# Projecting both heads of a chunk in one matmul against a block diagonal omega of 128 by 256

## The chip, the cores and the metric

The kernel runs on one core of a Trainium2 chip. The metric is the device time of one execution in microseconds (us), from the first to the last instruction and what the launch adds around them. Engines are named as in the profile: PE is TensorE doing matmuls, PEld its weight loads, DVE is VectorE, ACT is ScalarE, POOL is GpSimd and SP is the sync engine, which here only issues DMAs.

## The reference

Two stages follow each other. The first is linear attention with positive random features: 8 batches, 8 heads, 576 positions, head dimension 64, 128 features. The second is a gated feed-forward layer over the 4608 tokens (model width 512, hidden width 1536), which takes the attention's output as its input.

```python
def phi(x):                                # x is q or k, scaled by 1/sqrt(sqrt(64))
    proj = np.einsum('bhsd,md->bhsm', x, omega)      # 64 -> 128 features
    sq = np.sum(x * x, axis=-1, keepdims=True) / 2.0
    h = proj - sq
    h = h - np.max(h, axis=-1, keepdims=True)
    return np.exp(h) / np.sqrt(m)
kv = einsum('bhsm,bhsd->bhmd', phi(k), v);  z = phi(k).sum(axis=2)
num = einsum('bhsm,bhmd->bhsd', phi(q), kv)
den = einsum('bhsm,bhm->bhs', phi(q), z) + 1e-6
x = (num / den), heads side by side        # 4608 x 512
out = (silu(x @ w_gate) * (x @ w_val)) @ w_out
```

## The kernel before, in words

**Groups, steps, chunks.** The attention works on groups. A group is 256 rows (two chunks of 128, `CH = 2`) of two neighbouring heads of one batch, of q or of k. There are 72 groups of k and 72 of q. A step takes two groups, so there are 72 steps: six with k alone, sixty with one of q and one of k, six with q alone. Heads of one pair lie side by side: after the transposes, `x[:, i, ...]` has the 64 dimensions of the pair's first head in partitions 0 to 63 and those of its second head in partitions 64 to 127.

**What one step does to its two groups.** `load` brings the rows (L369, L376). `st_transpose` turns four chunks of 128 by 128 on PE (L411), squares the rows on POOL (L418) and copies the result to `x` on ACT (L419). `st_project` multiplies by omega (L434): for each group `i`, chunk `c` and head `hh` one matmul whose weights are 64 rows of `x` and whose moving operand is 64 rows of `omT`, 128 columns wide. That is eight matmuls a step in plain fp32. `omT` holds omega's transpose twice, once in partitions 0 to 63 and once in 64 to 127 (L337 to L348), so the first head uses the array's upper 64 rows and the second its lower 64 rows. The results go to two PSUM banks of 512 columns: `pp0` takes the first head of both groups, `pp1` the second head. In the profile each fp32 matmul shows as two weight loads and two matmul records, so a step has 16 records on L434.

`st_max` takes the sum of squares (L448) and, for each bank, the largest of 128 features (L455), both on DVE, and forms the bias in two small operations (L457, L458). `st_exp` writes `ph`, eight exponentials of 128 by 128 on ACT (L470), with a bias per row. A step's exponentials therefore wait for both maxima.

After that, k's `ph` is multiplied with v into `kvacc` (L572, two steps later), and q's `ph` is transposed (L596) and multiplied with the sums (`q_mult` L613, or in later batches `q_out` L653, whose weights are 64 columns wide and whose moving operand has 256 columns). `q_out` also transposes the finished rows in the early batches (L646).

**What sets the order.** The calls of a step are written out in two lists: `CLOSE`, for the steps before the first two tiles of 512 tokens are whole, and `GROUPED`, after that, in which pieces of the feed-forward layer (`SHARE`) stand between the attention's calls. The feed-forward's matmuls are in fp32r with 512 columns: gate and value L689, down L698, and in the last part, in a seven-product scheme, L928. A planner decides by fixed costs how much of it is given to each step. The order that an engine finally gets is made when the program is built, by a scheduler that may move an instruction past others of its engine. Weights of the feed-forward are converted by ACT and POOL (L251, L252, L277 to L295) beside it.

**PSUM.** Eight banks: three for `ps_moe`, two for `pp` (`ps_proj`), one each for the transposes (`ps_tr`), for the products (`ps_att`) and for `kvacc`. In odd early steps `pp` is taken from `ps_moe`.

Of the kernel before, what the change touches and what calls it, by code (L numbers as in the profile page):

```python
# [11 lines left out]
F32 = mybir.dt.float32  # L12
# [3 lines left out]
AF = mybir.ActivationFunctionType  # L16
ALU = mybir.AluOpType
AX = mybir.AxisListType
# [5 lines left out]
def kernel(  # L24
# [11 lines left out]
    nc = tc.nc  # L36
    B, H, S, D = q.shape
    M = omega.shape[0]
    NT, DM = out.shape
    DF = w_gate.shape[1]  # L40
    P = 128
# [6 lines left out]
    CH = G // P  # L48
# [4 lines left out]
    SCALE = 1.0 / math.sqrt(math.sqrt(D))  # L53
# [27 lines left out]
    const = ctx.enter_context(tc.tile_pool(name="const", bufs=1))  # L81
# [25 lines left out]
    def ps_moe(name, shape):  # L107
        return ps_m.tile(shape, F32, name=name, tag="m")
# [228 lines left out]

    omT = const.tile([P, M], F32, name="omT")  # L340

    def setup_omega():
        om2 = accp.tile([P, 2, D], F32, name="om2", tag="acc")
        for j in range(2):
            nc.scalar.dma_start(om2[:, j, :], omega)
        pt = ps_moe("pt_om", [P, M])
        nc.tensor.transpose(pt, om2.rearrange("p a d -> p (a d)"), ident)
        nc.scalar.activation(omT, pt, AF.Copy, scale=SCALE)  # L348

# [71 lines left out]
    def st_project(n):  # L423
        if n >= NS:
            return
        x, st, sq = sts[n]

        new = ps_moe if n < EARLY and n % 2 else ps_proj
        pp = [new(f"pp{hh}_{n}", [P, 2, CH, M]) for hh in range(2)]
        for i in range(2):  # L430
            for c in range(CH):
                for hh in range(2):
                    r = slice(hh * D, (hh + 1) * D)
                    nc.tensor.matmul(  # L434
                        pp[hh][:, i, c, :], x[r, i, c * P : (c + 1) * P], omT[r], start=True, stop=True
                    )
        sts[n] = st, sq, pp
        return True

# [2 lines left out]
    def st_max(n):  # L442
        if n >= NS:
            return
        st, sq, pp = sts[n]

        with tc.issue_after(biased[0].ins) if biased else ExitStack():
            nc.vector.tensor_reduce(  # L448
                st[:, 0].rearrange("p i c h -> p (i c h)"),
                sq.rearrange("p i c h d -> p (i c h) d"),  # L450
                axis=AX.X,
                op=ALU.add,
            )
        for hh in range(2):
            nc.vector.tensor_reduce(st[:, 1, :, :, hh], pp[hh], axis=AX.X, op=ALU.max, negate=True)  # L455
        s0, s1, s2, s3 = (st[:, j].rearrange("p i c h -> p (i c h)") for j in range(4))
        nc.vector.scalar_tensor_tensor(s2, s0, SQC, s1, op0=ALU.mult, op1=ALU.add)  # L457
        biased[:] = [nc.vector.scalar_tensor_tensor(s3, s0, -SQC, s2, op0=ALU.mult, op1=ALU.add)]  # L458
        step_end["v"] = biased[0]
        return True  # L460

    def st_exp(n):
        if n >= NS:
            return
        st, _, pp = sts.pop(n)
        for i, (kind, b, g) in enumerate(steps[n]):
            ph = att.tile([P, CH, 2 * M], F32, name=f"ph{i}_{n}", tag=f"ph{i}", bufs=3)
            for hh in range(2):
                for c in range(CH):
                    step_end["s"] = nc.scalar.activation(  # L470
                        ph[:, c, hh * M : (hh + 1) * M], pp[hh][:, i, c, :],
                        AF.Exp, bias=st[:, 3, i, c, hh : hh + 1], scale=1.0,
                    )
            box[kind, b, g] = ph
        return True
# [591 lines left out]
    def give(us):  # L1067
# [16 lines left out]
    SHARE = None  # L1084
    CLOSE = (
        st_project,
        q_norm,
        q_out,
        lambda n: st_transpose(n + 1),
        q_mult,  # L1090
        lambda n: k_accumulate(n, 0),
        st_max,
        q_transpose,
        lambda n: k_accumulate(n, 1),
        st_exp,
        q_den,
    )
    GROUPED = (
        q_out,
        st_project,  # L1100
        q_transpose,
        lambda n: k_accumulate(n, 0),
        lambda n: k_accumulate(n, 1),
        st_max,
        st_exp,
        q_den,
        lambda n: st_transpose(n + 1),
# [10 lines left out]
    for n in range(2):  # L1118
        load(n)
        if n == 0:  # L1120
            setup_omega()
# [64 lines left out]
```

## Time and profile before

| | |
|---|---|
| median of 3 runs | 1171.24 us (1169.88 to 1176.55) |
| the profiled execution | 1174.65 us, of which its span is 1172.6 us |
| PE busy, and weight loads | 1145.0 us (98%), 948.3 us (81%) |
| DVE, ACT, POOL busy | 703.3, 684.7, 588.6 us |
| first and last projection matmul | 6.4 and 546.4 us |

How to read the profile: a record of PE covers a matmul from its start to its modelled end, and matmuls overlap in the pipeline. So what a matmul costs PE is not its duration but how much later the next one starts. The timeline merges neighbouring records of one line and tile into one row: its first number is the start of the first, its second the time from there to the end of the last, and x16 says how many were merged. The distance from one row's start to the next row's start is then what the whole row took of PE. "64*128" in a PE row is the weights' rows and columns, "64x128" the moving operand's rows and columns. The column PEclk of the stages is the granted clock, 1.00 for full.

### The profile page before, as it was taken

The numbers are of one execution on the slowest core, as the hardware profiler recorded it, in microseconds if no ns is written. First come the engines' busy times: TensorE is split into PE (matmuls) and PEld (weight loads), VectorE is DVE, ScalarE is ACT, GpSimd is POOL, SyncE is SP. The second block draws the span as 40 slices with busy tenths as digits, with TensorE's granted clock in tenths as the row PEclk, the third lists the DMA queues.
The fourth block names the chain that finished last, engine by engine and source line by source line (L and its number), as shares of the span: only waits on it lengthen the run. The fifth ranks groups of instructions, "written<-read, shape, count | busy, mean of one in ns | idle before, by whom it ended". The sixth has DMA issues, their size and how long they took to land.

```text
span 1172.6 us, 18833 instructions
## 1 busy us (share of the span) xinstructions
PE 1145.0 (98%) x6633; PEld 948.3 (81%) x6633; DVE 703.3 (60%) x1266; ACT 684.7 (58%) x1541; POOL 588.6 (50%) x515
## 2 busy tenths in 40 slices
PE   8999999999999999999999999999999999999998
PEld 7888778888787778767778788888878888888886
DVE  3777576454666665556373566666566666456654
ACT  4888887877766866857434544444444445444441
POOL 3332353253656775586335655544455543555551
PEclk9999999999999999999999999999999999999999
DMA  6655355654445543431445111124211111211103
GB/s 141 160 135 132 102 161 142 185 151 122 129 130 139 143 140 102 109 86 55 135 109 151 57 55 55 54 65 124 63 50 46 52 52 46 81 55 54 46 18 72
DMA packets 173965, 114.30 MB, mean 97 GB/s; under 512 B 125840, under 2 KB 144304, under 8 KB 173872
## 3 DMA queue, kind: packets, MB, share of 16 engines
q1 hardware_dynamic: 172528, 112.78, 35.1%
q8 instruction: 52, 0.85, 0.3%
q10 hardware_dynamic: 1344, 0.33, 0.1%
q14 instruction: 41, 0.34, 0.1%
HBM read 87.88 MB, written 25.18 MB: 96 GB/s over the span
## 4 chain that ended last, share of the span: by engine, by line
PE 80%; DVE 7%; ACT 4%; POOL 3%; DMA 3%; issue 2%; SPq 0%; POOLq 0%; DVEq 0%; ACTq 0%
PE o L698 22%; PE a L928 16%; PE c L928 8%; PE g L689 6%; PE pp L434 6%; PE kvacc L572 5%; PE v L689 4%; PE d L928 4%; PE pt L411 3%; PE po L613 3%; PE ptq L596 2%; ACT ph L470 2%; PE xt L653 1%; POOL wlo L252 1%; PE xt L646 1%
## 5 line engine op out<-in xcount | busy, mean ns | idle before, releaser
L470 ACT ACTIVATE ph<-pp,st 128x128 f32<-128x128 f32 x576 | 157.3, 387 | 12.8 <-DVE st L458 12.3
L728 DVE TENSOR_TENSOR acc<-o,acc 128x512 f32<-128x512 f32 x156 | 105.8, 685 | 94.6 <-PE o L698 94.2
L418 POOL TENSOR_TENSOR sq<-nat 128x512 f32<-128x512 f32 x72 | 78.1, 1084 | 156.2 <-DVE st L448 113.5
L915 POOL TENSOR_TENSOR wlo<-wspare,whi 128x512 fp32r<-128x512 f32 (+1 forms) x60 | 60.9, 1036 | 117.4 <-ACT whi L914 111.0
L455 DVE TENSOR_REDUCE st<-pp 128x4 f32<-128x512 f32 x144 | 92.8, 683 | 43.2 <-PE pp L434 42.8
L434 PE MATMUL pp<-omT,x 64*128 64x128 f32 x1152 | 96.0, 296 | 3.4 <-ACT x L419 2.3
L252 POOL TENSOR_TENSOR wlo<-wraw,whi 128x512 fp32r<-128x512 f32 x59 | 82.5, 1404 | 26.9 <-ACT whi L251 23.0
L434 PEld LDWEIGHTS pp<-omT,x 64*128 64x128 f32 x1152 | 78.2, 195 | 20.8 <-issue 10.1
L915 POOL TENSOR_TENSOR wlo<-s,whi 128x512 fp32r<-128x512 f32 x64 | 82.4, 1306 | 3.8 <-ACT whi L914 3.8
L1024 ACT COPY late<-a 128x512 f32<-128x512 f32 x72 | 42.2, 586 | 60.0 <-PE a L928 58.8
L698 PE MATMUL o<-whi,late 128*128 128x512 f32 x192 | 74.5, 389 | 0.0
L572 PE MATMUL kvacc<-v,ph 128*128 128x65 f32 x512 | 69.1, 276 | 0.0
L536 DVE TENSOR_REDUCE dj<-jk 128x4 f32<-128x512 f32 x36 | 24.6, 684 | 73.3 <-POOL jk L532 60.7
L572 PEld LDWEIGHTS kvacc<-v,ph 128*128 128x128 f32 x512 | 66.4, 200 | 0.5
L789 POOL TENSOR_TENSOR hl<-sl,hh 128x512 fp32r<-128x512 f32 x36 | 46.9, 1306 | 34.6 <-ACT hh L788 34.6
L291 POOL TENSOR_TENSOR wc<-st 128x512 int32<-128x512 int32 x36 | 37.4, 1040 | 47.7 <-ACT st L289 25.2
L419 ACT COPY x<-pt 128x512 f32<-128x512 f32 x72 | 43.2, 600 | 28.3 <-PE pt L411 26.9
L689 PE MATMUL g<-xh,whi 128*128 128x512 f32 x144 | 59.5, 414 | 0.0
L1028 DVE TENSOR_TENSOR late<-c,late 128x512 f32<-128x512 f32 x25 | 17.3, 692 | 69.7 <-PE c L928 60.6
L698 PE MATMUL o<-whi,hh 128*128 128x512 f32 x144 | 58.4, 406 | 0.5 <-ACT sl L765 0.4
L689 PE MATMUL v<-xh,whi 128*128 128x512 f32 x144 | 57.7, 401 | 0.0
L689 PE MATMUL g<-xh,wlo 128*128 128x512 f32 x144 | 57.4, 398 | 0.0
(255 smaller groups left out, 3355.7 us busy)
## 6 DMA issues: line engine op xcount, KB each, us to landing
wraw<-wscr SPq DMA_DIRECT2D x63, 256.0 KB, 2.7
wspare<-wscr SPq DMA_DIRECT2D x60, 256.0 KB, 2.7
wscr<-wc SPq DMA_DIRECT2D x36, 256.0 KB, 2.2
out_dram<-acc SPq DMA_DIRECT2D x72, 128.0 KB, 2.4
nat<-in_k_dram SPq DMA_DIRECT2D x64, 128.0 KB, 3.0
nat<-in_q_dram SPq DMA_DIRECT2D x64, 128.0 KB, 3.1
v<-in_v_dram SPq DMA_DIRECT2D x62, 128.0 KB, 3.6
st<-in_moe_w_gate_dram SPq DMA_DIRECT2D x12, 512.0 KB, 3.9
```

The costliest lines, as they stand in the source:

```text
L252: nc.gpsimd.tensor_tensor(lo, raw, hi.bitcast(F32), op=ALU.subtract)
L418: nc.gpsimd.tensor_tensor(sq, nat, nat, op=ALU.mult)
L434: nc.tensor.matmul(pp[hh][:, i, c, :], x[r, i, c * P : (c + 1) * P], omT[r], start=True, stop=True)
L455: nc.vector.tensor_reduce(st[:, 1, :, :, hh], pp[hh], axis=AX.X, op=ALU.max, negate=True)
L470: step_end["s"] = nc.scalar.activation(ph[:, c, hh * M : (hh + 1) * M], pp[hh][:, i, c, :], AF.Exp, bias=st[:, 3, i, c, hh : hh + 1], scal ...
L572: nc.tensor.matmul(acc[:, 2 * (pr % 2) + hh, :], ph[:, c, hh * M : (hh + 1) * M], vt[:, 2 * c + j if gr is None else c, hh, :], start=firs ...
L689: nc.tensor.matmul(ps, a_[:, ws], b_[:, c, :], start=n == 0, stop=n == 3 * NC - 1)
L698: nc.tensor.matmul(ps, a_[:, ts_], b_, start=first and n == 0, stop=last and n == 2)
L728: nc.vector.tensor_tensor(a_, po, a_, op=ALU.add)
L789: nc.gpsimd.tensor_tensor(hl, h, hh.bitcast(F32), op=ALU.subtract)
L915: nc.gpsimd.tensor_tensor(lo, src_, hi.bitcast(F32), op=ALU.subtract)
L928: nc.tensor.matmul(ps, a_[:, w_], b_[:, c, :], start=start and c == 0 and m == 0, stop=c == CH - 1 and m == 2, skip_group_check=True,)
```

## The change

`omT` becomes a tile of 128 by 2 by 128: partitions 0 to 63 hold omega's transpose in the first 128 columns and zeros in the second, partitions 64 to 127 the other way round. One matmul with all 128 rows of `x` as weights and all 256 columns of `omT` then gives both heads' features of a chunk. A step has four such matmuls in place of eight. The banks are dealt out anew: `pp0` takes the first group and `pp1` the second, each with both chunks and both heads; the maxima (two, of the same size as before) and the exponentials (eight, the same) read them accordingly. The setup gets two memsets on DVE and one more small activation on ACT.

```diff
-    omT = const.tile([P, M], F32, name="omT")
+    omT = const.tile([P, 2, M], F32, name="omT")
...
-        nc.scalar.activation(omT, pt, AF.Copy, scale=SCALE)
+        for j in range(2):
+            r = slice(j * D, (j + 1) * D)
+            nc.vector.memset(omT[r, 1 - j], 0.0)
+            nc.scalar.activation(omT[r, j], pt[r], AF.Copy, scale=SCALE)
...
-        pp = [new(f"pp{hh}_{n}", [P, 2, CH, M]) for hh in range(2)]
+        pp = [new(f"pp{i}_{n}", [P, CH, 2, M]) for i in range(2)]
         for i in range(2):
             for c in range(CH):
-                for hh in range(2):
-                    r = slice(hh * D, (hh + 1) * D)
-                    nc.tensor.matmul(
-                        pp[hh][:, i, c, :], x[r, i, c * P : (c + 1) * P], omT[r], start=True, stop=True
-                    )
+                nc.tensor.matmul(
+                    pp[i][:, c].rearrange("p h m -> p (h m)"),
+                    x[:, i, c * P : (c + 1) * P],
+                    omT.rearrange("p h m -> p (h m)"),
+                    start=True, stop=True,
+                )
...
-        for hh in range(2):
-            nc.vector.tensor_reduce(st[:, 1, :, :, hh], pp[hh], axis=AX.X, op=ALU.max, negate=True)
+        for i in range(2):
+            nc.vector.tensor_reduce(st[:, 1, i], pp[i], axis=AX.X, op=ALU.max, negate=True)
...
-                        ph[:, c, hh * M : (hh + 1) * M], pp[hh][:, i, c, :],
+                        ph[:, c, hh * M : (hh + 1) * M], pp[i][:, c, hh, :],
```

Lines after the projection move down by three or four in the changed kernel (L434 becomes L435, L470 becomes L474, L596 becomes L600 and so on). The built order moves as follows at three places.

On PE, at step 41 in the grouped part: the transposes of finished rows (`xt`), the projection (`pp0_41`, `pp1_41`), the transposes of q's features (`ptq`), the k products (`kvacc`) and the transposes of the next step (`pt_42`). Before:

```order
L646 MATMUL xt3_5_3584<-ident_90,xn3_5_3562 128x128 x2
L434 MATMUL pp0_41_3593<-omT_96,x_41_3515 128x128
L434 MATMUL pp1_41_3594<-omT_96,x_41_3515 128x128
L434 MATMUL pp0_41_3593<-omT_96,x_41_3515 128x128
L434 MATMUL pp1_41_3594<-omT_96,x_41_3515 128x128
L434 MATMUL pp0_41_3593<-omT_96,x_41_3515 128x128
L434 MATMUL pp1_41_3594<-omT_96,x_41_3515 128x128
L434 MATMUL pp0_41_3593<-omT_96,x_41_3515 128x128
L434 MATMUL pp1_41_3594<-omT_96,x_41_3515 128x128
L596 MATMUL ptq3_7_3603<-ident_90,ph0_40_3500 128x128 x4
```

The same place on PE in the changed kernel:

```order
L650 MATMUL xt3_5_3423<-ident_90,xn3_5_3401 128x128 x2
L435 MATMUL pp0_41_3432<-omT_96,x_41_3354 128x256 x2
L435 MATMUL pp1_41_3433<-omT_96,x_41_3354 128x256 x2
L600 MATMUL ptq3_7_3438<-ident_90,ph0_40_3339 128x128 x4
L576 MATMUL kvacc5_0_3445<-v0_97,ph1_39_3243 128x65 x4
L414 MATMUL pt_42_3465<-ident_90,nat42_3206 128x128 x4
```

The neighbours stay; the eight matmuls that took turns between two banks become two on one bank and two on the other.

On PE, at step 18 in the close part, where the built order puts q's products (`po`) between a step's first projection matmul and its others. Before:

```order
L596 MATMUL ptq1_1_1244<-ident_90,ph0_16_1181 128x128 x4
L572 MATMUL kvacc2_0_1024<-v3_100,ph1_15_1116 128x65 x2
L434 MATMUL pp0_18_1267<-omT_96,x_18_1222 128x128
L613 MATMUL po1_0_1227<-kvr1_0_668,qt1_0_1177 128x65 x4
L434 MATMUL pp1_18_1268<-omT_96,x_18_1222 128x128
L434 MATMUL pp0_18_1267<-omT_96,x_18_1222 128x128
L434 MATMUL pp1_18_1268<-omT_96,x_18_1222 128x128
L434 MATMUL pp0_18_1267<-omT_96,x_18_1222 128x128
L434 MATMUL pp1_18_1268<-omT_96,x_18_1222 128x128
L434 MATMUL pp0_18_1267<-omT_96,x_18_1222 128x128
L434 MATMUL pp1_18_1268<-omT_96,x_18_1222 128x128
L646 MATMUL xt1_0_1283<-ident_90,xn1_0_1235 128x128 x2
```

The same place on PE in the changed kernel:

```order
L600 MATMUL ptq1_1_1175<-ident_90,ph0_16_1116 128x128 x4
L576 MATMUL kvacc2_0_967<-v3_100,ph1_15_1055 128x65 x2
L435 MATMUL pp0_18_1198<-omT_96,x_18_1153 128x256
L617 MATMUL po1_0_1158<-kvr1_0_631,qt1_0_1112 128x65 x4
L435 MATMUL pp0_18_1198<-omT_96,x_18_1153 128x256
L435 MATMUL pp1_18_1199<-omT_96,x_18_1153 128x256 x2
L650 MATMUL xt1_0_1210<-ident_90,xn1_0_1166 128x128 x2
```

The split stays, now after one of four matmuls instead of one of eight. In the program before, 55 of the 72 steps have their eight matmuls in one piece and 17 in two; in the changed one 61 have their four in one piece.

On ACT, at step 41: copies of finished rows and of transposed features (`xo`, `qt`), the copy of the next step's transposes (`x_42`), and the exponentials (`ph0`, `ph1`). Before:

```order
L668 COPY xo3_5_4_3590<-xt3_5_3584 128x192
L598 COPY qt3_7_3608<-ptq3_7_3603 128x512
L419 COPY x_42_3635<-pt_42_3630 128x512
L470 ACTIVATE ph0_41_3620<-pp0_41_3593,st_41_3516 128x128 x2
L470 ACTIVATE ph0_41_3620<-pp1_41_3594,st_41_3516 128x128 x2
L470 ACTIVATE ph1_41_3625<-pp0_41_3593,st_41_3516 128x128 x2
L470 ACTIVATE ph1_41_3625<-pp1_41_3594,st_41_3516 128x128 x2
```

The same place on ACT in the changed kernel:

```order
L672 COPY xo3_5_4_3429<-xt3_5_3423 128x192
L602 COPY qt3_7_3443<-ptq3_7_3438 128x512
L474 ACTIVATE ph0_41_3455<-pp0_41_3432,st_41_3355 128x128 x4
L474 ACTIVATE ph1_41_3460<-pp1_41_3433,st_41_3355 128x128 x4
L422 COPY x_42_3470<-pt_42_3465 128x512
```

The first group's exponentials now read one bank and the second's the other, and the copy of the next step's `x` stands behind the exponentials instead of ahead of them. From step 25 on that is so in nearly every step; in the steps up to 24 the copy stands ahead in both kernels.

## The prediction

> **What bounds the kernel now.** I read the page first: the busy shares, then the chain that ended last.
>
> ```profile
> PE 1145.0 (98%) x6633; PEld 948.3 (81%) x6633; DVE 703.3 (60%) x1266; ACT 684.7 (58%) x1541; POOL 588.6 (50%) x515
> PE 80%; DVE 7%; ACT 4%; POOL 3%; DMA 3%; issue 2%; SPq 0%; POOLq 0%; DVEq 0%; ACTq 0%
> ```
>
> PE is busy nearly throughout and makes up four fifths of the chain. That is an average over stages, so I cut the span at the first feed-forward matmul (about 119 us) and where the attention is done (about 575 us). The columns are each engine's busy time and record count, then the granted clock and the DMAs.
>
> ```profile
> 0.00:25.00 25.00, 19.45 (x114) 17.15 (x114) 8.80 (x18) 10.52 (x31) 7.99 (x25) 1.00 0.68 155
> 25.00:119.00 94.00, 92.23 (x894) 84.51 (x894) 70.33 (x188) 79.99 (x246) 31.14 (x30) 1.00 0.57 138
> 119.00:575.00 456.00, 441.95 (x3031) 359.53 (x3031) 265.76 (x564) 328.60 (x792) 253.02 (x223) 1.00 0.45 125
> 575.00:1172.00 597.00, 591.35 (x2600) 487.08 (x2598) 358.45 (x498) 265.59 (x474) 296.43 (x238) 1.00 0.24 68
> ```
>
> In the two stages that hold 68 of the 72 projections (25 to 575 us) PE idles 94.00 - 92.23 + 456.00 - 441.95 = 15.8 us in all. Work added to PE there must lengthen the run, but for what fits in those 15.8 us. So the question is what the projection takes of PE now and what it will take. This is its row among the groups, with the two waits of PE and PEld ahead of it that the change can touch:
>
> ```profile
> L434 PE MATMUL pp<-omT,x 64*128 64x128 f32 x1152 | 96.0, 296 | 3.4 <-ACT x L419 2.3 <-ACT ph L470 1.0
> PEld pp L434 <- ACT ph L470: 3.1, 6, 1.2
> ```
>
> A mean of 296 ns for 1152 records would be 341 us if they ran one after another, and the group is busy for 96.0. Records overlap, so durations don't price it; distances between starts do. Step 41, PE alone:
>
> ```profile
> 274.85 0.38 PE L646 MATMUL xt<-ident,xn 128*128 128x128 f32 x2
> 275.16 1.16 PE L434 MATMUL pp<-omT,x 64*128 64x128 f32 x16
> 276.25 0.66 PE L596 MATMUL ptq<-ident,ph 128*128 128x128 f32 x4
> ```
>
> Sixteen records take 276.25 - 275.16 = 1.09 us, 0.068 each. Step 18, with its split, gives the reference for full-array matmuls:
>
> ```profile
> 85.30 0.48 PE L434 MATMUL pp<-omT,x 64*128 64x128 f32 x2
> 85.71 1.10 PE L613 MATMUL po<-kvr,qt 128*128 128x65 f32 x8
> 86.75 1.16 PE L434 MATMUL pp<-omT,x 64*128 64x128 f32 x14
> 87.83 0.44 PE L646 MATMUL xt<-ident,xn 128*128 128x128 f32 x2
> 88.11 0.60 PE L411 MATMUL pt<-ident,nat 128*128 128x128 f32 x4
> 88.55 1.00 PE L572 MATMUL kvacc<-vrest,ph 128*128 128x65 f32 x8
> ```
>
> Four transposes with the same 128 moving columns take 88.55 - 88.11 = 0.44 us, 0.11 each. The projection's records come at 0.068 on average, and in step 18 its first two, one matmul of one head without a partner, take 85.71 - 85.30 = 0.41 us, almost as much as the four transposes. So two matmuls of 64 rows run at the same time when they stand next to each other, one in each half of the array: the two heads already share it. That is what the change replaces.
>
> **The change part by part.** *The projection before.* A whole block takes 1.09 us to the next row. Entering it costs something too: in step 41 the two L646 take 275.16 - 274.85 = 0.31 us where two such matmuls take 2 x 0.11, so 0.09 more; and behind the block the two L646 of step 18 take 88.11 - 87.83 = 0.28, so 0.06 more. A whole step is 1.09 + 0.09 + 0.06 = 1.24 us. Step 18's two pieces take 0.41 + (87.83 - 86.75 = 1.08) + 2 x 0.15 = 1.79 us.
>
> *The projection after.* Eight records of 128 rows and 256 columns, all different weights, one after another since each fills the array. The trace has no such form. From below: two records of 128 columns, 2 x 0.11 = 0.22 us. From above: matmuls of 512 columns in fp32r, which here stream a column once where an fp32 record seems to stream it twice; eleven distances in this row of starts give (328.65 - 326.16) / 11 = 0.226 us.
>
> ```profile
> 326.16 0.39 PE L689 MATMUL v<-xh,whi 128*128 128x512 f32 x1
> ...
> 328.65 0.39 PE L689 MATMUL v<-xh,wlo 128*128 128x512 f32 x1
> 328.97 0.65 PE L653 MATMUL xt<-qt,kvr 128*64 128x256 f32 x4
> 329.55 1.16 PE L434 MATMUL pp<-omT,x 64*128 64x128 f32 x16
> ```
>
> The one form with 256 fp32 columns is L653, here in its group's row:
>
> ```profile
> L653 PE MATMUL xt<-qt,kvr 128*64 128x256 f32 x128 | 20.4, 406 | 0.0
> ```
>
> It has 64-column weights; its four records run as two pairs, and the second pair starts about 0.65 - 0.41 = 0.24 us behind the first (0.41 being the mean duration). All three agree; I take 0.22, the row of the same data type and the whole array. A step is then 8 x 0.22 = 1.76 us. Weight loads are halved in number and each has 0.22 us of streaming to hide under; no gain from that, since weights of L434 are no bound now.
>
> *The sum on PE.* The 55 whole steps gain 1.76 - 1.24 = +0.52 us each: +28.6. The 17 split ones lie between 0 (step 18: 1.76 against 1.79) and +0.52; I take step 18's and +1 for the milder splits. 25 blocks stand right behind an L653, which works in half arrays itself; the entry of 0.09 isn't saved there: +2.3. Together +31.9 us on the engine that sets the end.
>
> *The slow start.* The first four blocks run at half the pace, whatever PEclk says:
>
> ```profile
> 6.43 2.08 PE L434 MATMUL pp<-omT,x 64*128 64x128 f32 x16 [0.68 <-ACT x L419]
> 8.45 1.11 PE L411 MATMUL pt<-ident,nat 128*128 128x128 f32 x4
> 10.23 2.08 PE L434 MATMUL pp<-omT,x 64*128 64x128 f32 x16 [0.67 <-ACT x L419]
> ```
>
> 8.45 - 6.43 = 2.02 us against 1.09. Doubled, the new block is 3.5 us, so +1.5 per step, 1.0 more than counted. The next transposes queue behind the block and the next `x` behind them, so the first two are on the path: +2 us (0 if PE's fuller use ends the slow spell sooner, +4 if all four count).
>
> *Moved and freed.* The maxima of step 18, and what stands ahead of the first projection:
>
> ```profile
> 87.73 1.29 DVE L455 TENSOR_REDUCE st<-pp 128x4 f32<-128x512 f32 x2
> ```
>
> ```profile
> 4.52 0.28 ACT L348 ACTIVATE omT<-pt_om 128x128 f32<-128x128 f32 x1
> ...
> 5.80 0.59 ACT L419 COPY x<-pt 128x512 f32<-128x512 f32 x1 [1.00 <-PE pt L411]
> 6.27 0.69 DVE L448 TENSOR_REDUCE st<-sq 128x8 f32<-128x512 f32 x1 [6.27 <-POOL sq L418]
> ```
>
> Both maxima run 87.73 - 86.75 = 1 us after the block's start, back to back. The first group's bank will be complete after half the block, 0.88 us, and the second's after 1.76, so the first maximum starts as now, the second waits for its bank, and the bias comes some 0.3 us later. Behind it on DVE only that step's small operations and on ACT its eight exponentials wait; PE uses them two steps (k) or one (q) later. It is hidden as long as a step's PE time grows more (+0.5) than this chain (+0.3). The copy of `x` that goes behind the exponentials delays the next projection's input by their length, with the feed-forward pieces of the grouped part as cover. Dealing the banks by group frees the first bank four exponentials earlier, which can remove PE's waits for L470 (1.0 + 3.1 us in the rows above), and a longer block leaves later waits less to wait for: -4 us, with 0 and the whole idle time of 15.8 us as bounds. The setup's two memsets and further activation cost nothing: DVE is idle until 6.27 us, and ACT between 4.80 and 5.80.
>
> *Two rules of the Trainium skill.* By the row tiles that the rows above show at work, the change gives up an overlap. The page "TensorE: Matmul & The Clock Gate", Part 3, says just that: matmuls with few rows in different row groups run concurrently, and one of them alone takes as long as a full one; its table, read as an estimate, has 3.07 times for four tiles, so some 1.5 for two, which would make the block 16 x 0.11 / 1.5 = 1.17 us and the sum 4 us smaller. The trace's 1.09 decides. The page "TensorEngine Tiling (Array Packing)", Key Properties, speaks for the change: switching the tiling mode drains the array. The trace prices that at the 0.15 us counted above, less than the overlap is worth.
>
> *Total.* 31.9 + 2 - 4 = +30 us: the profiled execution's 1174.65 would become 1204.6 (its span 1172.6 and 2.05 us around it). It stands 3.4 us above the median of the runs, 1171.24; the same +30 there gives **1201 us**.
>
> **The rivals.** *A, faster: a record of 256 columns costs hardly more than one of 128.* The 0.11 us of a full-array fp32 record may be its weight load, not its streaming: L572 has 65 columns, and its eight records still take 1.00 us in step 18, so they come nearly as far apart. If streaming were so much cheaper, eight wide records would take 8 x 0.11 = 0.88 us a step, 63 us in all, against 55 x 1.24 + 17 x 1.7 - 2.3 = 95 now: -32, and 1139 us. It decides below 95 / 576 = 0.165 us a record. Against it stand the 0.24 of L653 and the 0.226 of L689. The "TensorE: Matmul & The Clock Gate" page, under Back-to-back issue gap, gives 131 ns for a stream of matmuls with 512 columns; as an estimate 576 x 0.131 = 75 us, so 1151. The trace has 0.226 for that very width. 4%.
>
> *B, slower still: the weights of the wide records don't load ahead.* Then each record pays part of a load as well. L653 allows 0.65 - 0.39 = 0.26 us, if its last record is as short as those of L689; by that a step is 2.1 us and the sum 576 x 0.26 - 95 = +55, 1224 us with the start and the waits. Against it: L689's distances of 0.226 hold with new weights for every record. 6%.
>
> *C, most of PE's idle time is filled:* waits for ACT and DVE in the attention vanish behind the longer blocks, -15.8 in place of -4, so 1189 us. For it: those waits follow projections or the copies behind them; against it: they are scattered and many come in steps whose other work doesn't move. 6%.
>
> That the change doesn't do what it says is excluded: the built program has 288 projection matmuls 256 columns wide in place of 576.
>
> **How the numbers follow.** Forecast 84%, A 4%, B 6%, C 6%. The forecast's own range: 0.226 in place of 0.22 is +3.5; the splits up to +4; the start -2 to +2; the waits -6 to +4. That is 1193 to 1214. C reaches down to 1189; the range is 1189 to 1214. A measurement of this kernel can tell about 0.5%, 5.9 us. Slower by more than that: forecast, B and C with little doubt, 94%. Faster: A, 4%. Between: 2%, for an A that only half holds.
>
> **What would show it.** Right: the projection's group has 576 records of form 128*128 128x256; a whole block takes 1.7 to 1.85 us from its start to the next row; the rows ahead of it and behind it keep 0.11 a record; the second L455 of a step starts about 0.9 us after the first instead of back to back; the stage after the attention keeps its length. Wrong: blocks of 0.9 us (A) or above 2 us (B), or blocks as forecast with the stages 25 to 575 us grown by less than 20 us (C).

## The result and the profile after

The changed kernel took 1202.84 us (median of 4 runs, 1200.05 to 1204.51) against 1173.34 (4 runs) for the kernel before: a ratio of 1.025, 95% interval 1.0209 to 1.029, some 29 us slower. The profiled execution took 1204.51 us, with a span of 1202.8.

The page after, busy shares and chain:

```profile
PE 1175.1 (98%) x6057; PEld 976.7 (81%) x6057; DVE 713.4 (59%) x1268; ACT 684.9 (57%) x1540; POOL 590.0 (49%) x515
PE 83%; DVE 9%; POOL 3%; ACT 2%; issue 2%; DMA 2%; SPq 0%; DVEq 0%; POOLq 0%; ACTq 0%
```

PE has 576 records fewer and 30.1 us more of busy time, which is about the growth of the span (30.2 us). The stages after, cut at the same events (first feed-forward matmul, end of the attention):

```profile
0.00:25.00 25.00, 18.76 (x90) 15.40 (x91) 10.33 (x23) 11.60 (x34) 8.00 (x25) 1.00 0.69 155
25.00:124.00 99.00, 96.66 (x719) 89.57 (x719) 74.48 (x187) 80.81 (x246) 32.09 (x30) 1.00 0.53 129
124.00:600.00 476.00, 464.32 (x2636) 381.30 (x2635) 271.26 (x561) 324.67 (x784) 253.08 (x223) 0.99 0.43 119
600.00:1202.00 602.00, 595.40 (x2618) 490.40 (x2616) 357.33 (x498) 267.86 (x479) 296.80 (x238) 1.00 0.24 68
```

The attention grew from about 575 to 600 us; the cuts are round. PE still idles (99.00 - 96.66) + (476.00 - 464.32) = 14.0 us between 25 and 600, hardly less than the 15.8 before, and the third stage's granted clock reads 0.99. Both will matter. A block at step 41, PE alone, then one behind L657 (the L653 of before), then the two maxima of step 41 on DVE:

```profile
282.89 0.38 PE L650 MATMUL xt<-ident,xn 128*128 128x128 f32 x2
283.11 1.89 PE L435 MATMUL pp<-omT,x 128*128 128x256 f32 x8
284.84 0.60 PE L600 MATMUL ptq<-ident,ph 128*128 128x128 f32 x4
```

```profile
338.95 0.65 PE L657 MATMUL xt<-qt,kvr 128*64 128x256 f32 x4
339.53 1.99 PE L435 MATMUL pp<-omT,x 128*128 128x256 f32 x8
341.36 0.60 PE L600 MATMUL ptq<-ident,ph 128*128 128x128 f32 x4
```

```profile
284.18 0.69 DVE L459 TENSOR_REDUCE st<-pp 128x4 f32<-128x512 f32 x1 [2.38 <-PE pp L435]
285.04 0.69 DVE L459 TENSOR_REDUCE st<-pp 128x4 f32<-128x512 f32 x1 [0.17 <-PE pp L435]
```

The eight wide records take 284.84 - 283.11 = 1.73 us, 0.216 each, where 1.76 was priced; behind L657 1.83. Entry and exit are gone: the two L650 take 0.22. The maxima start 0.86 us apart. And the change brought a wait that the kernel before did not have on PE:

```profile
PE xt L657 <- ACT x L422: 4.8, 3, 2.4
```

### The profile page after: what moved, and what is told of

It reads as the page before. It is cut to its first block, busy times and chain, and to the rows that moved or that the text cites. A ratio compares the mean times of both kernels' runs of the same rounds, so it can differ in the third digit from the quotient of the medians.

```text
span 1202.8 us, 17634 instructions
## 1 busy us (share of the span) xinstructions
PE 1175.1 (98%) x6057; PEld 976.7 (81%) x6057; DVE 713.4 (59%) x1268; ACT 684.9 (57%) x1540; POOL 590.0 (49%) x515
## 4 chain that ended last, share of the span: by engine, by line
PE 83%; DVE 9%; POOL 3%; ACT 2%; issue 2%; DMA 2%; SPq 0%; DVEq 0%; POOLq 0%; ACTq 0%
PE o L702 21%; PE a L932 15%; PE pp L435 10%; PE c L932 8%; PE g L693 6%; PE v L693 5%; PE kvacc L576 5%; PE d L932 4%; PE po L617 2%; PE pt L414 2%; PE ptq L600 2%; PE xt L657 1%; DVE st L459 1%; DMA first_b<-xs 1%; POOL jk L536 1%
## 5 line engine op out<-in xcount | busy, mean ns | idle before, releaser
L474 ACT ACTIVATE ph<-pp,st 128x128 f32<-128x128 f32 x576 | 158.3, 384 | 15.5 <-DVE st L462 14.1
L435 PE MATMUL pp<-omT,x 128*128 128x256 f32 x576 | 149.7, 402 | 1.7 <-ACT x L422 1.7
L459 DVE TENSOR_REDUCE st<-pp 128x4 f32<-128x512 f32 x144 | 97.7, 688 | 57.6 <-PE pp L435 56.8
L435 PEld LDWEIGHTS pp<-omT,x 128*128 128x128 f32 x576 | 107.2, 197 | 24.7 <-issue 5.4
L602 ACT COPY qt<-ptq 128x512 f32<-128x512 f32 x72 | 41.8, 589 | 44.5 <-PE ptq L600 44.1
L576 PE MATMUL kvacc<-v,ph 128*128 128x65 f32 x512 | 66.1, 268 | 0.0
L576 PEld LDWEIGHTS kvacc<-v,ph 128*128 128x128 f32 x512 | 63.4, 192 | 0.4 <-ACT kvr L490 0.3
```

The source lines that it names most:

```text
L435: nc.tensor.matmul(pp[i][:, c].rearrange("p h m -> p (h m)"), x[:, i, c * P : (c + 1) * P], omT.rearrange("p h m -> p (h m)"), start=True, ...
L459: nc.vector.tensor_reduce(st[:, 1, i], pp[i], axis=AX.X, op=ALU.max, negate=True)
L474: step_end["s"] = nc.scalar.activation(ph[:, c, hh * M : (hh + 1) * M], pp[i][:, c, hh, :], AF.Exp, bias=st[:, 3, i, c, hh : hh + 1], scal ...
L576: nc.tensor.matmul(acc[:, 2 * (pr % 2) + hh, :], ph[:, c, hh * M : (hh + 1) * M], vt[:, 2 * c + j if gr is None else c, hh, :], start=firs ...
```

## Experiments

The theory: two matmuls of 64 rows share the array, and the change gives that up; the rivals are the new dealing of the banks with the order that comes of it, and the width of 256 columns. The ratios are those to the kernel before, run on the same chip.

**Full rows, 128 columns.** The zeros stay, width, banks and the built order on PE are those of before.

```diff
-  pp[hh][:, i, c, :], x[r, i, c * P : (c + 1) * P], omT[r], ...
+  pp[hh][:, i, c, :], x[:, i, c * P : (c + 1) * P], omT[:, hh], ...
```

> As before, but each of the eight matmuls uses all 128 rows of x, against 128 columns of the block diagonal omega (one head's half, zeros included); banks, instruction count and the built order on PE are those of before. Theory (two heads share the array): the sharing is gone, sixteen records come 0.109 us apart, a block takes 1.75 to 1.85 us, and the time is that of the changed kernel, 1198 to 1206 us. Rival (the changed dealing of banks, or the built order that changes with it, costs the time): neither is changed here, so 1172 us, within 6. Rival (the width of 256 columns costs by itself): clearly below the changed kernel, 1180 to 1195 us.

Measured: 1194.9 us, ratio 1.0192 (1.0177 to 1.0207). Step 41 of this kernel:

```profile
281.86 1.95 PE L436 MATMUL pp<-omT,x 128*128 128x128 f32 x16
283.64 0.60 PE L598 MATMUL ptq<-ident,ph 128*128 128x128 f32 x4
```

The sixteen records take 283.64 - 281.86 = 1.78 us, 0.11 each. With order and banks untouched most of the 29 us is there, so the lost sharing is the main cause. But some 7 us are missing against the changed kernel, and the width does not explain them: a block takes 1.73 us there, 0.05 less than here. I had not expected a remainder.

**The heads one after the other.** 64 rows and the old banks, but neighbours use the same half.

```diff
-        for i in range(2):
-            for c in range(CH):
-                for hh in range(2):
+        for hh in range(2):
+            for i in range(2):
+                for c in range(CH):
```

> As before, 64 rows and the same banks, but the four matmuls of the first head come first and then the four of the second, so that neighbours use the same half of the array. Theory (sharing): records come 0.11 us apart instead of two per 0.11, the block goes from 1.09 to about 1.76 us and still pays its entry and exit of 0.15: 72 times 0.67 less some waits, 1210 to 1222 us, slower than the changed kernel. Rival (banks or built order): banks are as before, so 1172 us, within 6, or what the new order does, in either direction, with records still 0.068 us apart.

Measured: ratio 1.0519 (1.0502 to 1.0537), some 1233 us: the right direction, and above the upper end. A second run was to say why.

> The kernel with the heads one after the other once more, for a profile of an undisturbed run; it took 1233 us where I had expected 1210 to 1222. Theory (blocks of 1.64 us as priced, +0.55 a whole step and 40 us in all, and on top of it a late rise of the clock, since half of the array is kept idle): the early projection blocks last 2.5 us or more well beyond the 25 us of the kernel before, and the later ones 1.64. Rival (the block itself is dearer than priced): blocks above 1.8 us throughout.

Measured: 1245.91 us, ratio 1.0608 (1.0556 to 1.066). Two blocks of this run, early and late, on PE:

```profile
70.98 3.09 PE L434 MATMUL pp<-omT,x 64*128 64x128 f32 x16
74.00 0.69 PE L646 MATMUL xt<-ident,xn 128*128 128x128 f32 x2
...
248.35 1.71 PE L434 MATMUL pp<-omT,x 64*128 64x128 f32 x16
249.99 0.66 PE L596 MATMUL ptq<-ident,ph 128*128 128x128 f32 x4
```

The late block takes 1.64 us, 0.10 a record, against 1.09 with nothing changed but the order of the eight matmuls: that is the sharing, seen alone. At 71 us a block still takes 3.02 us, the slow pace that the profiled kernel before leaves behind by 26 us, and from 143.8 us on the granted clock is 0.50 for another 20.5 us. So the overshoot is time at half pace and not a dearer block.

**Banks dealt by chunk.** The changed kernel with `pp[c][:, i, hh, :]` in place of `pp[i][:, c, hh, :]`.

> The changed kernel with the banks dealt by chunk instead of by group: matmuls take turns between two banks again, and no bank is complete or free early. Theory (sharing): the time of the changed kernel, 1203 us, or up to 4 more, since I credited 4 us to the early free bank. Rival (dealing of banks costs the time): a good part of the 30 us comes back, 1175 to 1190 us.

Measured: 1195.89 us, ratio 1.0202 (1.0186 to 1.0217). The dealing does not carry the loss, but the early free bank brought no 4 us either: without it the kernel is 7 us faster. Its trace has one stretch of half clock behind 25 us, the changed kernel's has three. That led to the next pair.

**The copy of x put back.** In the changed kernel:

```diff
         st_max,
+        lambda n: st_transpose(n + 1),
         st_exp,
         q_den,
-        lambda n: st_transpose(n + 1),
...
+                    with tc.issue_after(copied[0].ins) if n >= EARLY else ExitStack():
                         step_end["s"] = nc.scalar.activation(ph[...], pp[i][:, c, hh, :], AF.Exp, ...)
```

> The changed kernel with the copy of the next step's x put back ahead of the exponentials on ACT from the grouped part on (the transposes that it needs are called earlier, and the exponentials are issued behind it). Theory (7 us of the changed kernel's 30 are not the wide block: PE waits up to 2.4 us for this copy in front of L657, and after such a wait the clock falls to half for 3.4 us): those waits and at least two of the three slow stretches go, 1193 to 1199 us. Rival (the difference to the kernels with other banks is the chip's, or chance): as the changed kernel beside it, within 3 us.

> The changed kernel itself, on the chip of the kernels beside it. If the 7 us that it takes over the kernel with the banks dealt by chunk belong to the program: 1200 to 1205 us again, with two or three stretches of half clock in its records after 25 us. If they were that chip's or chance: 1193 to 1198 us.

Measured: 1189.95 us, ratio 1.0149 (1.012 to 1.0177), and beside it the changed kernel once more 1201.13 us, ratio 1.0248 (1.0221 to 1.0276). The changed kernel's time is its own, and 11 us of it go with this edit. The mechanism, in the changed kernel's trace (ACT and PE):

```profile
403.78 0.64 ACT L422 COPY x<-pt 128x512 f32<-128x512 f32 x1
...
404.46 0.65 PE L657 MATMUL xt<-qt,kvr 128*64 128x256 f32 x4 [1.91 <-ACT x L422]
...
405.05 3.68 PE L435 MATMUL pp<-omT,x 128*128 128x256 f32 x8
...
408.53 0.63 PE L600 MATMUL ptq<-ident,ph 128*128 128x128 f32 x4
```

`x` is copied out of the bank of `ps_tr`, and in the later batches `q_out` writes its result to the same bank. With the copy behind eight exponentials PE stands for 1.91 us. Then the block behind it takes 408.53 - 405.05 = 3.48 us, twice its price. The window of that block, with the granted clock 0.50 ahead of the last two columns:

```profile
405.20:408.60 3.40, 3.40 (x9) 2.58 (x10) 1.72 (x4) 2.50 (x5) 2.10 (x3) 0.50 0.46 112
```

With the copy first, the same two stages read as follows, and no wait of PE for this copy in front of `xt` is left:

```profile
25.00:123.00 98.00, 95.68 (x716) 88.80 (x714) 74.05 (x186) 80.06 (x244) 31.64 (x30) 1.00 0.53 129
123.00:587.00 464.00, 458.26 (x2626) 377.32 (x2626) 265.03 (x561) 325.02 (x783) 252.77 (x223) 1.00 0.44 122
```

PE's idle time falls from 14.0 to (98.00 - 95.68) + (464.00 - 458.26) = 8.1 us, and the clock stays at 1.00: 6 us of waits and three stretches of 3.4 us at half pace, 1.7 us lost in each, are the 11 us. Two of the three stretches stand behind waits for this copy, which end at 404.46 and 554.24 us. The third stands behind a wait of 2.42 us for `kvr`, the copy of the sums (L490), which ends at 453.02 us. It goes with the edit too (the longest wait for that copy is then 1.0 us), but why is not shown.

**The same edit in the kernel before** (`pp[hh][:, i, c, :]` kept):

> The kernel before with the copy of the next step's x held ahead of the exponentials from the grouped part on, the edit that took 11 us off the changed kernel. Theory (that edit mends a place that only the changed order had: the kernel before has the copy ahead in 61 of 71 steps already and one stretch of half clock behind a wait): 0 to 4 us gained, 1168 to 1172 us. Rival (the copy is late in the kernel before as well, and the edit is worth about as much there): 1160 to 1165 us.

Measured: 1175.51 us, ratio 1.0026 (0.9998 to 1.0055). Nothing gained: the place was a consequence of the change.

**Each projection matmul twice.** In the kernel before, and in the changed one (`for _ in range(2):` around the matmuls):

> The kernel before with every projection matmul issued twice into the same place. Theory (sharing): eight more pairs a step at 0.111 us, 0.89 us, on a PE that sets the end: 72 times 0.89 = +64 us, less 0 to 8 us of waits that they fill, 1228 to 1237 us. If the overlap were only one of records and the array worked one after the other, +125 us, 1297. If PE's idle time took most of the additional work, below 1215 us.

> The changed kernel with every projection matmul issued twice into the same place. Theory (PE sets the end; a wide record is 0.216 us): eight more records a step, 72 times 1.73 = +124 us on the changed kernel's 1203, less 0 to 6 us of waits, 1321 to 1328 us. If the waits of the attention hid part of the wide block, less: below 1310 us.

Measured: 1221.27 us, ratio 1.0418 (1.0397 to 1.0439), and 1308.61 us, ratio 1.1143 (1.1102 to 1.1184). A block of each, on PE:

```profile
304.47 2.06 PE L433 MATMUL pp<-omT,x 64*128 64x128 f32 x32
306.46 0.66 PE L595 MATMUL ptq<-ident,ph 128*128 128x128 f32 x4
```

```profile
299.73 3.62 PE L436 MATMUL pp<-omT,x 128*128 128x256 f32 x16
303.19 0.60 PE L601 MATMUL ptq<-ident,ph 128*128 128x128 f32 x4
```

The blocks are as priced: 1.99 - 1.09 = 0.90 us for eight more pairs, 3.46 - 1.73 = 1.73 for eight more wide records. The times are below what I expected, +49 instead of +64 and about +106 instead of +124 over the changed kernel. Additional PE work doesn't arrive in full, since it fills waits: PE's idle time falls by 9 us in the pairs and by 11 in the wide blocks (against the changed kernel's second run). In the trace of the pairs half pace also ends earlier than in that of the kernel before, and a slow stretch which that one has at 523.5 us is not there.

**Whole blocks.** The kernel before, with the projection issued behind the last queued `po`:

```diff
+        with tc.issue_after(po_end[0].ins) if po_end else ExitStack():
             for i in range(2):          # the eight matmuls
```

> As before, but a step's projection is issued only behind the products po that are already queued, so that 69 of 72 steps have their eight matmuls in one piece instead of 55. Theory (a split costs entries and exits of the shared mode, and a lone matmul has no partner): fourteen splits at 0.35 to 0.55 us go, -5 to -8 us, less what the projection now waits for po, so 1165 to 1169 us. Rival (a split costs nothing, since step 18's total equals the wide block): no change, within 2 us.

Measured: 1172.23 us, ratio 0.999 (0.9973 to 1.0008). A miss. Only three of the 17 splits are left, and from the fifth block on the projection takes 3.7 us less, but PE waits 6.0 us more; in this kernel

```profile
PE xt L648 <- DVE xn L625: 4.2, 6, 1.2
```

where the kernel before has 1.1 us in one wait. What the splits cost they seem to have saved in waits.

**A warmer start.** The kernel before with ten additional 128 by 128 matmuls in the first steps:

```diff
+    def warm(name, count):
+        wt = ps_moe(name, [P, P])
+        for _ in range(count):
+            nc.tensor.matmul(wt, ident, ident, start=True, stop=True)
```

> The kernel before with eight additional matmuls of 128 by 128 (identity by identity, into a bank that nothing reads) in PE's idle time before and behind the first transposes, and two in a later step. Theory (how early the clock rises from half to full depends on how full the array is kept; full-array programs had it at 10 to 16 us, this one at 25): full clock by about 12 us, 2 to 6 us gained, 1166 to 1170 us. Rival (the start is bound by loads and by the chain from step to step): no change within 2 us, or 1 to 3 us lost to the additional matmuls.

Measured: 1179.81 us, ratio 1.0064 (1.0044 to 1.0085), slower. Two windows of its start:

```profile
7.20:17.40 10.20, 7.29 (x79) 6.21 (x79) 6.20 (x14) 5.85 (x20) 3.04 (x3) 1.00 0.63 138
17.40:37.90 20.50, 19.33 (x109) 17.72 (x108) 6.75 (x15) 8.29 (x29) 4.19 (x5) 0.50 0.57 140
```

Full clock came early, as hoped; PE then ran ahead of its loads, was busy for 7.29 of 10.20 us, and the clock fell to half for 20.5 us. The gain was given back, and more.

**The projection in fp32r.** The changed kernel with `omT` and `x` as fp32r tiles, one record per matmul.

> The changed kernel with the projection's operands in fp32r, which drops digits of x and omega that the kernel before keeps: part of the computation is changed. Theory (an fp32 matmul is two records that each stream their columns twice): one record per matmul that streams once, four a step at 0.11 to 0.12 us, a block of 0.46 us: 72 times 1.3 us less than the changed kernel, plus 5 to 15 us of waits that PE's shorter steps lay bare, 1114 to 1124 us, below the kernel before. Rival (the wide form pays for its weight loads, not for streaming): four records at 0.2 us, 1140 us or more.

Measured: 1157.28 us, ratio 0.9873 (0.9838 to 0.9907). The only kernel here that is faster than the one before, with fewer digits in the projection. A block and the two stages:

```profile
292.73 0.72 PE L435 MATMUL pp<-omT,x 128*128 128x256 f32 x4
293.29 0.60 PE L600 MATMUL ptq<-ident,ph 128*128 128x128 f32 x4
```

```profile
25.00:114.00 89.00, 80.41 (x566) 75.61 (x566) 64.98 (x161) 67.91 (x211) 29.34 (x27) 0.84 0.55 134
114.00:557.00 443.00, 421.76 (x2518) 344.55 (x2518) 273.58 (x580) 338.22 (x815) 255.29 (x224) 0.99 0.48 131
```

The block takes 0.56 us, 0.14 a record, so one record per matmul holds, somewhat dearer than the 0.11 to 0.12 us expected. But PE idles for 8.6 + 21.2 = 29.8 us and runs the first of these stages at a mean clock of 0.84. The blocks save 72 x (1.73 - 0.56) = 84 us and the time falls by 46 from the changed kernel's: almost half of what the block gave up went into waits and slow stretches, and the result is 33 us or more short of the 1114 to 1124 that I expected.

## Why the prediction was right, and where it was not

The total was right, 1201 us forecast and 1202.84 measured, and so was the main term, the array. That the total is within 2 us is in part luck: the copy, the waits and the start were all off, and their errors cancel.

To see the terms apart, take the profiled executions, 1172.6 and 1202.8 us long, between two marks: the start of the fifth projection block (26.49 us before, 24.77 in the changed kernel, 23.59 with the copy first) and the start of the projection's last record (546.37, 576.92 and 563.22 us). Between the marks the change adds 32.3 us, and with the copy first 19.8.

*The sharing and its price: right.* Two heads run at once in the two halves; heads apart cost 1.64 us a block, full rows 0.11 a record, whatever the banks. The sum of +31.9 us on PE nearly holds. I added up the distances between starts, without the idle time, from the kernel before to the one with the copy first: between the marks the projection takes 39.8 us more, and the attention's other matmuls, which lose entries and exits, take 11.3 less. That is +28.5 us for 68 steps, where the sum has 31.9 - 4 x 0.52 = +29.8.

*The slow start: not settled.* I gave it +2 us, on top of 4 x 0.52 = 2.1 for the four steps. The first blocks of the changed kernel, on PE:

```profile
12.43 3.77 PE L435 MATMUL pp<-omT,x 128*128 128x256 f32 x8 [0.67 <-ACT x L422]
...
17.76 1.95 PE L435 MATMUL pp<-omT,x 128*128 128x256 f32 x8
19.54 0.60 PE L414 MATMUL pt<-ident,nat 128*128 128x128 f32 x4
```

The second block takes the doubled 3.5 us, but the third is at full pace, 19.54 - 17.76 = 1.78 us, while the profiled kernel before crept until after the fourth. So the changed kernel reaches the fifth block 1.7 us earlier instead of 4.1 later. But this does not show that the change ends the slow spell sooner. The kernel before with the copy's edit has the same matmuls on PE in the same order in these steps, and its trace reads:

```profile
10.29 1.16 PE L435 MATMUL pp<-omT,x 64*128 64x128 f32 x16 [0.67 <-ACT x L420]
11.38 0.66 PE L412 MATMUL pt<-ident,nat 128*128 128x128 f32 x4
...
20.95 1.16 PE L435 MATMUL pp<-omT,x 64*128 64x128 f32 x16
```

Here pairs are at full pace from the second block on, and the fifth starts at 20.95 us. The changed kernel's second run is at full pace from the second block as well and starts its fifth at 22.67 us. So the moment differs between executions of the same steps, and the profile of the kernel before is a late one. Between the two early traces the change costs 1.7 us.

*Filled waits: too small.* With the copy first PE's idle time falls from 15.8 to 8.1 us, -8 where I took -4 (-7.2 of it between the marks). Another -1.8 is a slow stretch from 523.5 to 526.9 us that the kernel before has behind a wait of 1.89 us, and that I did not count. In the changed kernel itself PE's idle time is 14.0 us, because a new wait took the place of the filled ones.

*The moved copy: the step that failed.* "The copy of `x` that goes behind the exponentials delays the next projection's input by their length, with the feed-forward pieces of the grouped part as cover": the next projection was indeed covered, but I looked only at who reads `x`. The copy also empties a bank, and `q_out`, which stands ahead of the projection, waits for that bank. I priced it at nothing; putting it back gains 11 us in the runs and 32.3 - 19.8 = 12.5 between the marks, of which 4.8 us are waits for this copy and 2 x 1.7 the slow stretches right behind them.

So the 30.2 us between the two profiles are about +28.5 for the array, -9 for waits and the slow stretch, +12.5 for the copy with what goes with it, and -2 for the start and the end; the forecast's +30 was +31.9, -4, 0 and +2. The array and the copy are shown by runs, the waits are read from the traces, and the start's share belongs to these two executions.

*The rivals.* A and B fell with the blocks of 1.73 us. C, the rival on waits, was half right: about 8 of the 15.8 us of waits are filled once the copy is first. That the time is then 1190 us, near C's 1189, is chance, since the start and the slow stretch make up the rest. The last stage kept its length, and the second maximum starts 0.86 us behind the first, as expected.

*Left open.* The kernel with full rows has the old order and no stretch of half clock behind 25 us, and still takes 5 us more than the one with the copy first. Most of that is in its blocks, whose median is 1.84 us against 1.78. With the banks by chunk the copy stands behind the exponentials as well; there the wait at 404 us is missing, and one of 2.38 us that ends at 546.83 us is followed by full clock. Why the first is missing, I did not try.

## What to carry to other kernels

Matmuls that fill half of the array's rows are not waste where a partner for the other half stands next to them; before merging two, look at the distance between starts and not at the number of instructions. When a scheduler moves a copy out of PSUM, ask who writes that bank next, not only who reads the copy. A wait of PE of some 2 us can cost nearly as much again in slow clock behind it. And before a difference at the start is put down to a change, look at another execution of the same steps.

## What the runs showed of the hardware

When PE leaves half pace at the start differs between executions of the same steps. With pairs the first block at full pace was the second (10.29 us), the third (14.57, whole blocks) or the fifth (26.49, the kernel before), with the same matmuls on PE up to there; with the wide blocks it was the second (12.11, the second run) or the third (17.76). With one half of the array at a time a block at 71 us was still at half pace, though PE was busy for all of the 50.0 us from 25 to 75. The profile's clock column reads 1.00 in this first stretch; only the distances between records tell.

Behind a wait the clock can fall to half for 3.4 us, or for a multiple: 20.5 us in the warm start is six times that. The Trainium skill's page "TensorE: Matmul & The Clock Gate", Part 1, has a monitor that works in windows of 3.4 us and halves the clock after an idle one; the lengths agree. It warns of idle gaps above about 3.4 us. Here a wait of 1.91 us ahead of L657 at 404 us was enough, with PE busy for 3.4 us at half pace right behind it.

The length of the wait alone does not decide. With the copy first PE waits 2.39 us ahead of L602, until 575.86 us, and the clock stays at 1.00:

```profile
574.70:578.10 3.40, 2.24 (x12) 1.95 (x13) 0.18 (x1) 1.97 (x4) 3.40 (x4) 1.00 0.48 129
578.10:581.50 3.40, 3.40 (x18) 2.54 (x16) 0.69 (x1) 0.62 (x1) 2.84 (x3) 1.00 0.63 184
```

In the changed kernel the slow stretches start at 405.17, 452.96 and 555.36 us, 14 and 30 times 3.413 us apart. Laid out from each trace's first change of clock, such a division holds all of the 1.91 us at 404 us, but an edge at 574.66 us cuts the wait of 2.39 us into two halves of 1.2 us. I infer that the idle time within one division counts; no run varies it by itself. Nor is it all: in the kernel before with the copy's edit a slow stretch at 47.29 us stands behind a division with only 0.67 us of idle time.

A wide fp32 block behind the matmuls of L657, whose weights have 64 columns, takes 0.1 us more, all of it on its first record (1.83 against 1.73 us); behind the whole-array transposes of L650 nothing of the kind is seen.
